# Attention with cluster masks, then token mixing, on one core: last sums read first, late weights cast earlier, first maxima moved

## The chip, the cores and the metric

The kernel runs on one core of one Trainium2 chip. A core has five engines that each work through their own queue in order: TensorE (PE, with its weight loads as PEld), VectorE (DVE), ScalarE (ACT), GpSimd (POOL) and SyncE (SP), which here issues nearly all DMAs. The metric is the device time of one execution in microseconds. Times in the text are microseconds unless marked otherwise.

## What is computed

Two steps, the second on the output of the first. B = 4, H = 8 heads, S = 768 tokens, D = 64, 16 clusters, so the second step has a model width of 512.

```python
q_assign = argmax(q_n . c_n);  k_assign = argmax(k_n . c_n)      # cluster of each query and key
mask   = q_assign[:, :, :, None] == k_assign[:, :, None, :]
scores = where(mask, scale * q @ k.T, -1e9)
attn   = exp(scores - max(scores));  attn /= sum(attn) + 1e-9
x      = (attn @ v) as [B, S, 512]

theta  = x @ w_theta
yr     = einsum('ts,bsd->btd', w_tok_r, x * cos(theta))
yi     = einsum('ts,bsd->btd', w_tok_i, x * sin(theta))
u      = x + yr + yi
out    = u + maximum(u @ w_ch, 0)
```

## The kernel before, in words

**Precision.** Large products are made from a high and a low part. A ScalarE copy rounds a tensor to its high part (`hi`, type fp32r), GpSimd or VectorE subtracts it from the whole for the low part (`lo`), and TensorE adds three products: hi by hi, hi by lo, lo by hi. The weights arrive as 64-bit floats and are turned into 32-bit ones first (`to_f32`, L124): one ScalarE operation (L142), then four on VectorE (L144, L147, L150, L153). `split_w` (L157) does that and the split (L165, L166).

**Attention.** A pair is two heads of one batch on the two halves of the partitions; there are 16 pairs, `NPAIR`. A unit `u` is one block of 128 keys against one half (384) of the queries, for both heads `j` of the pair; a pair has 12 units, 192 in all (`NUT`). For each unit: `score_products` makes the scores on TensorE (L408, four products: three of the split and one with the mask rows `mk`, `mq`), `exps` takes the exponential on ScalarE (`at`, L471), `add_exps` sums on GpSimd (L482), and `weighted` multiplies by `v` (L543). Ten units ahead (`LEAD`) `max_products` computes whole rows of scores (tile `m`, two PSUM buffers, one for each head) and `max_of` takes their maximum on VectorE (`nm`, L430); `shift_row` brings it into a row of `mq` by a small DMA (L451). `interleave` issues several lists of products in turn, `both` makes the two heads' products in turn and then calls a function for each head.

The cluster of each token is found per pair: logits (L286), turned (`lt`, L299), maximum and one-hot code on VectorE, turned back (`ot`, L327). Pairs 0 and 1 do that ahead of the loop. `keep_up(n)` issues n small matmuls that compute nothing anybody reads (L228, tile `idle`); `WAIT` gives their numbers at five places: ahead of and behind the turn of the centroids (L254, L256), ahead of the turns of the logits (L724), ahead of the one-hot codes (L731) and ahead of the loop (L760).

The end of a pair has two generators, driven by unit numbers. `sums` (L499) adds up the exponentials by a product with a column of ones (tile `sm`, L510), reads the result (for the last pair `last_sum`, VectorE, L518, tile `se`), sends it through DRAM and back, takes the reciprocal (L528) and loads it broadcast (`rb`). `normalise` (L560) multiplies the pair's output by it (L564, for the last two pairs on VectorE) and stores it. Pair `pi` has its steps at units `12 pi + 12 + SUMS` and `12 pi + 12 + NORM`. So the last product of sums (pair 15) stands at unit 196, and pair 14 is normalised at units 193 and 196.

**Token mixing.** A tile is 128 tokens of a batch, 6 in each, 24 in all. `theta(b, t)` computes the angles (tile `tp`, L643), reduces them modulo 2 pi on VectorE (`rotation_reduce`: `kk` L648, `r` L649 and L650), takes cosine and sine on ScalarE and multiplies by x (L911, L913), and splits the results into `zhc, zlc, zhs, zls` (ScalarE L916, GpSimd L918). `mix` adds the tile's products with the token weights into six PSUM banks `y` (L967). A tile's `theta` is written two tiles ahead of its `mix` (`AHEAD`). After the sixth tile of a batch `channel` adds x (`add_y`, L978, split at L980 and L981) and multiplies by `w_ch` (`channel_out`, tiles `cp` and `cy`, L990). x as rows arrives by `xb` loads (L631), one buffer, turned on VectorE (L636).

The token weights of row blocks 0 to 2 are ready in split form from the attention stage. Those of blocks 3 to 5 are kept in DRAM as 32-bit floats, and `w_ch` (blocks c0 to c3) is converted in the second stage. The generator `late` (L870) does both; the loop over tiles takes one step of it in each of the six tiles of batch 0. The block casts (L878) are held behind a split that `weights_after` names, and all their temporary tiles are the four buffers of tag `u` that `add_y` uses later.

**What sets the order.** In the attention stage the order on every engine is the program's, tied by hand with `in_order` (L673). In the second stage a planner orders each engine's queue by program order and by times that it estimates, except where `behind(x)` or `issue_after` holds an instruction behind x on the same engine. The second stage's PSUM pools (`pm` with two banks, `py` with the six y banks) take over the banks of the attention's pools, the one of the last `sm` among them.

Of the kernel before, what the change touches and what calls it, by code (L numbers as in the profile page):

```python
# [23 lines left out]
TAIL = 2  # L24
NEXT = 6
FILL = 5
WAIT = (37, 10, 11, 28, 14)
SUMS = (4, 6, 8, 9, 10)
NORM = (13, 16)
TERMS = 3  # L30
# [4 lines left out]
INV_2PI = float(1.0 / (2.0 * math.pi))  # L35
# [8 lines left out]
def kernel(  # L44
# [19 lines left out]
    nc = tc.nc  # L64
# [3 lines left out]
    NT = S // P  # L68
# [156 lines left out]
    def keep_up(n, over=None):  # L225
        over = idle if over is None else over
        for _ in range(n):
            nc.tensor.matmul(over[:, 0:P], lhsT=busy, rhs=busy, start=True, stop=True)  # L228
# [174 lines left out]
    def interleave(*lists):  # L403

        for x in zip(*lists):
            for j, (out, stat, cols, mov, over, start, stop) in x:
                r = slice(64 * j, 64 * j + 64)
                nc.tensor.matmul(out, lhsT=stat[r, cols], rhs=mov[r, over], start=start, stop=stop)  # L408

    def max_products(u, j):  # L410

        pi, a, i = split_u(u)
        s = st[pi]
        if i == 0 and ("nm", a) not in s:
            s["nm", a] = p2.tile([P, 2, NH], F32, tag="nm", name=f"nm{u}")
        t = a * NH + i // 2
        m = s["m", j] = m_tile(f"m{u}_{j}")
        q = slice(t * P, (t + 1) * P)
        res = []
        for c in range(2):  # L420
            k = slice(c * HS, (c + 1) * HS)
            res.append((j, (m[:, c, 0:HS], s["hq"], q, s["hk"], k, True, False)))
            res.append((j, (m[:, c, 0:HS], s["mq"], q, s["mk"], k, False, True)))
        return res

    def max_of(u, j):

        pi, a, i = split_u(u)
        s = st[pi]
        nc.vector.tensor_reduce(  # L430
            out=s["nm", a][:, j, i // 2:i // 2 + 1], in_=s["m", j][:, :, 0:HS], op=ALU.max, axis=AX.XY,
            negate=True)
# [55 lines left out]
    def both(products, u, then, *banks):  # L488
        interleave(*(products(u, j, *banks) for j in range(2)))
        for j in range(2):  # L490
            then(u, j)
# [68 lines left out]
    def normalise(pi):  # L560
        b, p = divmod(pi, NP)
        s = st.pop(pi)

        (nc.gpsimd if pi < NPAIR - 2 else nc.vector).tensor_tensor(  # L564
            out=s["xt"], in0=s["xt"], in1=s["rb"], op=ALU.mult)
        yield
        nc.sync.dma_start(out=xT_d[b][:, p], in_=s["xt"].rearrange("p a s -> p (a s)"))
# [13 lines left out]
    def run(gen):  # L581
        for _ in gen:
            pass
# [28 lines left out]
    def behind(x):  # L612
        return tc.issue_after(x.ins) if x is not None else nullcontext()
# [31 lines left out]

    def rotation_reduce(n, name, tp, kk, r):

        nc.vector.tensor_scalar_mul(kk, tp, INV_2PI)  # L648
        nc.vector.scalar_tensor_tensor(out=r, in0=kk, scalar=-C1, in1=tp, op0=ALU.mult, op1=ALU.add)  # L649
        nc.vector.scalar_tensor_tensor(out=r, in0=kk, scalar=-C2, in1=r, op0=ALU.mult, op1=ALU.add)  # L650
        ab = ma[n % 2].tile([P, DM], F32, tag="ab", name=f"ab{name}")
        with behind(first_sin[0] if n == 1 else None):
            nc.scalar.activation(out=ab, in_=r, func=AF.Abs)
        return ab
# [7 lines left out]
    def stages(units, gen):  # L662

        for u in units:
            at_unit(u, lambda: next(gen, None))
        at_unit(units[-1] + 1, run, gen)
# [95 lines left out]
    for pi in range(NPAIR):  # L762
        u = NU * pi
        if pi > 0:
            prepare(pi, g2 if pi == 2 else assign(pi))
            at_unit(u - NU + 7, load_v, pi)
        for a in range(2):
            if pi or a:
                at_unit(u + a * NT - LEAD + NT, shift_row, pi, a)
        if pi < NPAIR - 1:  # L770
            for a in range(2):
                at_unit(7 if pi == a == 0 else u + ADDS[a], add_sums, pi, a)
        stages([u + NU + k for k in SUMS], sums(pi))
        stages([u + NU + k for k in NORM], normalise(pi))
    for x, gen in enumerate(early_weights()):
        units = [W_EVERY * x + k for k in W_UNITS]
        stages(units if units[-1] < NUT else W_LAST[x % (NPAIR - 1)], gen)
# [4 lines left out]
    u = 0  # L782
    while u <= NUT or todo:
        start = len(nc.cur_bb.bb.instructions)
        ahead = u + LEAD

        def pieces(u):
            for x in sorted(x for x in todo if x <= u):
                for fn, a in todo.pop(x):
                    fn(*a)  # L790

        if 0 <= u < NUT:
            both(score_products, u, exps)
            if u == 0:
                for n, x in ((1, "mk"), (0, "mq")):
                    nc.scalar.activation(
                        out=st[1][x], in_=turn_one_hot(1, n), func=AF.Identity,
                        **(dict(scale=BIG, bias=mbi) if n else {}))
                nc.gpsimd.memset(cl["q"], -100.0)
                keep_up(NEXT)  # L800
                both(max_products, ahead - 2, max_of)
                keep_up(2 * NEXT)
            add_exps(u)
            if ahead < NUT:
                scores_beside_max(u + 1, ahead, 0)
        pieces(u - 0.5)
        if 0 < u <= NUT:
            weighted(u - 2)
            if u == NUT:
                keep_up(FILL, m_tile("fill")[:, 0])  # L810
            weighted(u - 1)
            if ahead >= NUT:
                weighted_out(u - 1)
        pieces(u)
        if 0 <= u < NUT:
            if ahead < NUT:
                scores_beside_max(u + 1, ahead, 1)
            else:

                both(score_products, u + 1, exps, *([m_tile(f"sc{u + 1}")] if u < NUT - 6 else []))  # L820
            add_exps(u + 1)
        if 0 < u and ahead < NUT:
            weighted_out(u - 1)
        pieces(u + 1)
        in_order(start)
        u += 2
# [43 lines left out]
    def late():  # L870

        for t in range(EARLY, NT):
            for w, x in ((w_r, "r"), (w_i, "i")):
                hi, lo = w[t]
                kept = u_tile("kept").rearrange("p c s -> p (c s)").bitcast(F32)[:, 0:S]
                nc.sync.dma_start(out=kept, in_=w_d[t, x])
                with behind(weights_after[0]):
                    nc.scalar.copy(out=hi, in_=kept)  # L878
                nc.gpsimd.tensor_tensor(out=lo, in0=kept, in1=f(hi), op=ALU.subtract)
            if t < NT - 1:  # L880
                yield
        for c in range(NCT):
            if c:
                yield
            for gen in split_w(*w_c[c], w_ch[c * P:(c + 1) * P], DM, wt_pair, nc.gpsimd, CK):
                run(gen)

    zs, splits = {}, []

# [209 lines left out]
```

## Time and profile before

| what | value |
|---|---|
| runs of the kernel, median (lowest to highest) | 792.14 (790.19 to 792.31) |
| the profiled execution: device time | 791.57 |
| the profiled execution: span of its instructions | 789.8 |
| mean granted TensorE clock | 0.996 |
| DMA queue share of 16 engines | 30.7% |

The profile was taken on one execution; its span runs from the first to the last instruction, and its device time is a little longer. A row of the timeline gives start, duration, engine, line and operation, with `out<-in`, the shapes, and the number of instructions merged in it; the bracket at the end is the idle time of that engine just before and what ended it. A row of the waits gives who waited for whom, the total, how often, and the longest. A row of the windows gives the length, then the busy time and count of PE, PEld, DVE, ACT and POOL, the granted TensorE clock (1.00 is full), the share of the DMA engines and the GB/s.

The stages lie as follows: start up to about 24, attention up to about 446, mixing from 453, the channel product of batch 0 from 519 to 539 and that of batch 1 from 606 to 623.

### The profile page before, as it was taken

What the parts mean: (1) busy time and instruction counts of PE and PEld (TensorE: products, weight loads), DVE (VectorE), ACT (ScalarE), POOL (GpSimd) and SP (SyncE); (2) the same over time, 40 slices, a digit from 0 to 9 for tenths busy, and PEclk for the clock granted to TensorE, in tenths of its full rate; (3) what the DMA queues carried; (4) which work ended last, traced back from release to release, by engine and by line L of the source; (5) the groups of instructions that cost most, each with busy time, mean ns of one, the idle gap of its engine ahead of it and who ended that gap; (6) DMA issues with size and microseconds to landing.
All of it is one profiled execution on the core that took longest, in us unless ns stands there. A gap on an engine that the chain in (4) does not pass through costs nothing.

```text
span 789.8 us, 14483 instructions
## 1 busy us (share of the span) xinstructions
PE 779.1 (99%) x5624; PEld 577.9 (73%) x5624; DVE 570.7 (72%) x689; ACT 387.8 (49%) x780; POOL 496.2 (63%) x289
## 2 busy tenths in 40 slices
PE   9999999999999999999999899999999999999998
PEld 7666565566565666656665588888889988899998
DVE  6689999999999999999899668754444433633322
ACT  3465756576767676666655445432333123403310
POOL 3468888989999999988987475451216022332231
PEclk9999999999999999999999999999999999999999
DMA  4113314431443234433463575115111411030001
GB/s 142 37 64 99 113 54 133 132 112 66 149 133 113 89 125 139 127 106 127 132 206 105 133 217 152 21 21 173 17 23 28 160 28 27 15 94 14 1 21 61
DMA packets 81708, 73.24 MB, mean 93 GB/s; under 512 B 59544, under 2 KB 65512, under 8 KB 81256
## 3 DMA queue, kind: packets, MB, share of 16 engines
q1 hardware_dynamic: 81634, 72.32, 30.7%
q8 instruction: 44, 0.72, 0.4%
q14 instruction: 24, 0.20, 0.1%
q10 hardware_dynamic: 6, 0.00, 0.0%
HBM read 56.89 MB, written 15.31 MB: 91 GB/s over the span
## 4 chain that ended last, share of the span: by engine, by line
PE 82%; DVE 10%; DMA 3%; issue 2%; ACT 2%; SPq 1%; DVEq 0%; ACTq 0%
PE sc L408 24%; PE y L967 19%; PE av L543 15%; PE tp L643 6%; PE cy L990 5%; PE m L408 4%; PE cp L990 3%; DMA xb<-xT_d 2%; PE sm L510 1%; PE lg L286 1%; PE idle L228 1%; DVE nm L430 1%; PE y L990 1%; DVE acc L486 1%; PE lt L299 1%
## 5 line engine op out<-in xcount | busy, mean ns | idle before, releaser
L471 ACT ACTIVATE at<-sc 128x384 f32<-128x384 f32 x384 | 173.7, 493 | 99.8 <-PE sc L408 50.8
L430 DVE TENSOR_REDUCE nm<-m 128x1 f32<-128x768 f32 x192 | 179.7, 945 | 21.9 <-PE m L408 19.2
L482 POOL TENSOR_TENSOR acc<-at,at 128x768 f32<-128x768 f32 x64 | 129.0, 2016 | 36.7 <-ACT at L471 33.6
L408 PE MATMUL m<-hk,hq 64*128 64x384 f32 x384 | 146.8, 385 | 0.8 <-DVE nm L430 0.6
L543 PE MATMUL av<-at,vt 128*64 128x384 f32 x768 | 145.3, 499 | 0.2 <-ACT xt L558 0.2
L918 POOL TENSOR_TENSOR zlc<-ab,zhc 128x512 fp32r<-128x512 f32 x24 | 32.3, 1345 | 169.3 <-ACT zhc L916 165.8
L482 POOL TENSOR_TENSOR acc<-acc,at 128x768 f32<-128x768 f32 x64 | 131.9, 2061 | 7.9 <-ACT at L471 5.7
L408 PE MATMUL m<-mk,mq 64*128 64x384 f32 x384 | 127.3, 334 | 0.0
L408 PE MATMUL sc<-hq,hk 64*128 64x384 f32 x384 | 117.0, 387 | 0.9 <-ACT at L471 0.9
L408 PEld LDWEIGHTS sc<-hq,hk 64*128 64x128 f32 x384 | 56.1, 183 | 61.7 <-issue 24.9
L408 PE MATMUL sc<-lq,hk 64*128 64x384 f32 x384 | 98.1, 335 | 0.0
L408 PE MATMUL sc<-mq,mk 64*128 64x384 f32 x384 | 98.0, 335 | 0.0
L408 PE MATMUL sc<-hq,lk 64*128 64x384 f32 x384 | 97.8, 334 | 0.0
L543 PEld LDWEIGHTS av<-at,vt 128*64 128x64 f32 x768 | 46.5, 136 | 58.5 <-issue 53.6
L408 PEld LDWEIGHTS m<-hk,hq 64*128 64x128 f32 x384 | 70.1, 183 | 3.1 <-DVE nm L430 2.3
L408 PEld LDWEIGHTS m<-mk,mq 64*128 64x128 f32 x384 | 70.7, 185 | 0.2 <-DVE mk L714 0.2
L648 DVE TENSOR_SCALAR kk<-tp 128x512 int32<-128x512 f32 x24 | 16.4, 684 | 73.4 <-PE tp L643 73.2
L486 DVE TENSOR_TENSOR acc<-acc,acc 128x768 f32<-128x768 f32 x30 | 68.9, 2295 | 0.0
L616 ACT CAST xh<-xT 128x512 fp32r<-128x512 f32 x23 | 14.3, 620 | 99.1 <-PE tp L643 99.1
L981 POOL TENSOR_TENSOR ul<-xT,uh 128x384 fp32r<-128x384 f32 (+1 forms) x36 | 33.5, 960 | 37.2 <-ACT uh L980 35.5
L408 PEld LDWEIGHTS sc<-mq,mk 64*128 64x128 f32 x384 | 55.1, 184 | 0.0
L408 PEld LDWEIGHTS sc<-lq,hk 64*128 64x128 f32 x384 | 55.1, 185 | 0.0
(174 smaller groups left out, 1728.0 us busy)
## 6 DMA issues: line engine op xcount, KB each, us to landing
vt<-in_v_dram SPq DMA_DIRECT2D x16, 384.0 KB
rb<-sd SPq DMA_DIRECT2D x32, 192.0 KB
xT_d<-xt SPq DMA_DIRECT2D x16, 384.0 KB
xb<-xT_d SPq DMA_DIRECT2D x96, 64.0 KB
rawq<-in_qT_dram SPq DMA_DIRECT2D x15, 384.0 KB
rawk<-in_kT_dram SPq DMA_DIRECT2D x15, 384.0 KB
w<-in_wrT_dram SPq DMA_DIRECT2D x6, 768.0 KB
xT<-xT_d SPq DMA_DIRECT2D x3, 1536.0 KB
```

The costliest lines, as they stand in the source:

```text
L408: nc.tensor.matmul(out, lhsT=stat[r, cols], rhs=mov[r, over], start=start, stop=stop)
L430: nc.vector.tensor_reduce(out=s["nm", a][:, j, i // 2:i // 2 + 1], in_=s["m", j][:, :, 0:HS], op=ALU.max, axis=AX.XY, negate=True)
L471: last_exp[0] = nc.scalar.activation(out=s["at", a, i][:, j], in_=s["sc", j], func=AF.Exp, scale=SCALE)
L482: last_acc[0] = nc.gpsimd.tensor_tensor(out=s["acc", a, x], in0=prev, in1=at, op=ALU.add)
L486: nc.vector.tensor_tensor(out=s["acc", a, 0], in0=s["acc", a, 0], in1=s["acc", a, 1], op=ALU.add)
L543: nc.tensor.matmul(s["av"][64 * j:64 * j + 64], lhsT=s["vt"][:, i, j, :], rhs=s["at", a, i][:, j], start=(i == 0), stop=(i == NT - 1))
L643: nc.tensor.matmul(tp, lhsT=xx[:, c, :], rhs=w_th[c][k], start=(n == 0), stop=(n == 3 * NCT - 1))
L648: nc.vector.tensor_scalar_mul(kk, tp, INV_2PI)
L918: nc.gpsimd.tensor_tensor(out=zl, in0=tr, in1=zh.bitcast(F32), op=ALU.subtract)
L967: last_mix[0] = nc.tensor.matmul(y_at(b, d, c0, c1), lhsT=zz[:, d * P:(d + 1) * P], rhs=ww[:, c0:c1], start=first and lead, stop=last, ski ...
L981: nc.gpsimd.tensor_tensor(out=ul[:, d, :], in0=x, in1=uh[:, d, :].bitcast(F32), op=ALU.subtract)
L990: nc.tensor.matmul(cp, lhsT=w_c[d][k][:, e * P:(e + 1) * P], rhs=uu[:, d, :], start=(n == 0), stop=(n == 3 * NCT - 1), skip_group_check=True)
```

## The change

Five edits, in three places of the program.

- The end of attention: `kk` of token tile 1 is held behind `last_sum` on VectorE, and `normalise` of pair 14 moves four units later, to units 197 and 200, behind the last pair's product and its read at unit 196.
- The late weights: `late` yields at other points. Row blocks 3 and 4 come in tile 0 (before: 3 in tile 0, 4 in tile 1), block 5 and c0 in tile 1 (before tile 2), c1, c2 and c3 in tiles 2, 3 and 4 (before 3, 4 and 5), and tile 5 has none.
- The start: in unit 0 the maxima of unit 8 are issued right behind the first scores, one head after the other, ahead of the turns of pair 1's one-hot codes; before, they came behind those turns and were interleaved. The 6 + 12 filler matmuls around them go, and three numbers of `WAIT` fall: 10 to 4, 11 to 9 and 14 to 8.

```diff
-WAIT = (37, 10, 11, 28, 14)
+WAIT = (37, 4, 9, 28, 8)
...
-        nc.vector.tensor_scalar_mul(kk, tp, INV_2PI)
+        with behind(last_sum[0] if n == 1 else None):
+            nc.vector.tensor_scalar_mul(kk, tp, INV_2PI)
...
-        stages([u + NU + k for k in NORM], normalise(pi))
+        stages([u + NU + k + (4 if pi == NPAIR - 2 else 0) for k in NORM], normalise(pi))
...
             both(score_products, u, exps)
             if u == 0:
+                for j in range(2):
+                    interleave(max_products(ahead - 2, j))
+                    max_of(ahead - 2, j)
                 for n, x in ((1, "mk"), (0, "mq")):
                     nc.scalar.activation(
                         out=st[1][x], in_=turn_one_hot(1, n), func=AF.Identity,
                         **(dict(scale=BIG, bias=mbi) if n else {}))
                 nc.gpsimd.memset(cl["q"], -100.0)
-                keep_up(NEXT)
-                both(max_products, ahead - 2, max_of)
-                keep_up(2 * NEXT)
...
-            if t < NT - 1:
+            if t == NT - 2:
                 yield
         for c in range(NCT):
-            if c:
-                yield
             for gen in split_w(*w_c[c], w_ch[c * P:(c + 1) * P], DM, wt_pair, nc.gpsimd, CK):
                 run(gen)
+            yield
```

## The prediction

> **What bounds the kernel now.** I read the chain that ended last first, then TensorE's waits, and only then single stretches of the timeline. The page's part 4 by engine, and two rows of the waits of TensorE:
>
> ```profile
> PE 82%; DVE 10%; DMA 3%; issue 2%; ACT 2%; SPq 1%; DVEq 0%; ACTq 0%
> PE y L967 <- DVE se L518: 2.3, 1, 2.3
> PE cy L990 <- ACT uh L980: 1.3, 1, 1.3
> ```
>
> The end is set by TensorE: it is on 82% of the chain, and no other engine comes near it. So an edit is worth only what it takes off TensorE: an idle gap, a stretch at a low clock, or instructions. Two single gaps stand out, 2.3 us at the first token-mixing product and 1.3 us in the first channel product. They cost more than their length, as the granted clock (the figure before the DMA share) shows in one slice behind each:
>
> ```profile
> 454.00:455.00 1.00, 1.00 (x5) 0.81 (x4) 1.00 (x3) 0.97 (x3) 0.00 (x0) 0.50 1.02 406
> 523.00:524.00 1.00, 1.00 (x5) 1.00 (x4) 1.00 (x4) 0.92 (x4) 1.00 (x2) 0.50 0.09 16
> ```
>
> TensorE is fully busy in both slices, at half its clock. A gap here is paid twice, once idle and once slow.
>
> **Part 1: the last sums, and the multiplication kk of token tile 1 behind them.** TensorE and VectorE where attention ends and mixing begins, the start of the next tile's theta product, and a later mixing of one tile from the chain:
>
> ```profile
> 446.18 1.50 PE L510 MATMUL sm<-acc,ecol 128*32 128x384 f32 x16
> 447.43 2.05 DVE L564 TENSOR_TENSOR xt<-xt,rb 128x768 f32<-128x768 f32 x1
> 449.40 0.68 DVE L648 TENSOR_SCALAR kk<-tp 128x512 int32<-128x512 f32 x1
> 449.59 1.08 PE L643 MATMUL tp<-wth_hi,xl 128*128 128x512 f32 x4
> 452.30 0.54 DVE L518 TENSOR_SCALAR se<-sm 128x384 f32<-128x384 f32 x1
> 452.99 0.58 PE L967 MATMUL y<-wr_hi,zhc 128*128 128x512 f32 x2 [2.32 <-DVE se L518]
> 463.02 1.08 PE L643 MATMUL tp<-wth_hi,xh 128*128 128x512 f32 x4
> 542.03 8.41 PE y L967 x48
> ```
>
> The sums are ready at 446.18 + 1.50 = 447.68, but VectorE reads them (se) only at 452.30: normalise of pair 14 (2.05), kk and what hangs on it stand ahead. The PSUM banks of y lie over the attention's pools, so the first y waits for that read, although TensorE is free at 449.59 + 1.08 = 450.67. The change puts pair 14's normalise at units 197 and 200, behind the last product at unit 196, and kk behind se. Then se runs at about 447.9, or 0.7 to 1.2 later if an instruction of tile 3 is put in ahead; either way it is done before 450.67. The 2.32 of idle time goes, and the slow clock with it: mixing tile 0 takes 463.02 - 452.99 = 10.03 against 8.41 later on, 1.62 more. Gain 2.32 + 1.62 = 3.94. Bounds: 0 (another reader of those banks, or the low halves of tile 0, come as late as se) to 3.94.
>
> What is late next: the same VectorE work is still to be done, with se first. VectorE is free for it from 447.43 and has to wait for the sums, 0.3 to 0.5, and kk, r and all of tile 1's halves move back by that. TensorE meets tile 1 earlier:
>
> ```profile
> 458.36 1.30 POOL L918 TENSOR_TENSOR zls<-r,zhs 128x512 fp32r<-128x512 f32 x1
> 465.76 0.50 PE L967 MATMUL y<-wr_hi,zhc 128*128 128x512 f32 x2
> ```
>
> Tile 1's last half is done at 459.66, then about 460.1; its mixing starts at 465.76 - 3.94 = 461.8. That is 1.7 to spare, so I cost it at nothing. With that cover gone, each us late is a us, and about 1.6 of low clock on top.
>
> Here the Trainium skill ("TensorE: Matmul & The Clock Gate", the section on why this matters for your kernels) advises against idle gaps over about 3 us, since one idle window takes the clock back to half. The gaps of 2.32 and 1.30 above are shorter and still have 0.50 behind them, so the trace decides, and I give the rule no chance here; by it idle time alone would count, 2.32 + 1.30 + the 0.8 of part 3 = 4.4 and 787.7, in place of the sum below.
>
> **Part 2: the late weights.** Each of tiles 0 to 5 of batch 0 has a share of the late weights: before t3 / t4 / t5 and c0 / c1 / c2 / c3, after t3 and t4 / t5 and c0 / c1 / c2 / c3 / none (t: the two token weights of a row block, c: a block of w_ch). Nothing is added or removed; c1 to c3, t4, t5 and c0 come one tile earlier. The last tile before the channel product is then free. The channel product of batch 0 beside that of batch 1, with the VectorE work ahead of each:
>
> ```profile
> 511.51 1.40 DVE L147 TENSOR_SCALAR wtmp<-wtmp 128x512 int32<-128x512 int32 x1
> 517.44 0.74 DVE L978 TENSOR_TENSOR xT<-y,xT 128x384 f32<-128x384 f32 x2
> 518.78 0.51 PE L990 MATMUL cp<-uh,wch_hi 128*128 128x384 f32 x2
> 521.24 0.45 PE L990 MATMUL cy<-uh,wch_hi 128*128 128x384 f32 x1 [1.30 <-ACT uh L980]
> 539.10 1.08 PE L643 MATMUL tp<-wth_hi,xh 128*128 128x512 f32 x4
> 599.82 0.76 DVE L978 TENSOR_TENSOR xT<-y,xT 128x384 f32<-128x384 f32 x2
> 606.04 0.51 PE L990 MATMUL cp<-uh,wch_hi 128*128 128x384 f32 x2
> 622.70 1.08 PE L643 MATMUL tp<-wth_hi,xh 128*128 128x512 f32 x4
> ```
>
> In batch 1, which has no weights to convert, the first sum x + y (L978) starts 606.04 - 599.82 = 6.22 ahead of the channel product; in batch 0 only 518.78 - 517.44 = 1.34, because the conversion of c3 stands in VectorE's queue. So the casts uh come late, TensorE idles 1.30 and then runs slow. The same matmuls take 539.10 - 518.78 = 20.32 in batch 0 and 622.70 - 606.04 = 16.66 in batch 1. Without c3 there, batch 0 should look like batch 1: gain 3.66, bounds 0 and 3.66.
>
> What this crowds is tiles 0 to 2: ScalarE gets two casts and GpSimd two subtractions more right behind tile 1, on SP the loads for t5 and c0 wait for buffers that are freed there, and the xb loads of a later tile stand behind them. Tiles are made about two ahead of their mixing, which covers it; the case where it doesn't is the slower rival.
>
> **Part 3: the start.** Pair 0's first units, then what stands before them:
>
> ```profile
> 23.23 0.95 PE L228 MATMUL idle<-busy 128*128 128x128 bf16 x14
> 24.11 0.44 PE L408 MATMUL sc<-hq,hk 64*128 64x384 f32 x2
> 25.01 1.13 PE L327 MATMUL ot<-identb,clq 128*128 128x128 bf16 x12
> 25.86 0.90 ACT L796 ACTIVATE mk<-ot,mbi 128x768 fp32r<-128x768 bf16 x1
> 26.41 0.44 PE L408 MATMUL m<-hk,hq 64*128 64x384 f32 x2
> 27.32 0.84 PE L228 MATMUL idle<-busy 128*128 128x128 bf16 x12
> 28.09 0.44 PE L408 MATMUL sc<-hq,hk 64*128 64x384 f32 x1
> 28.43 0.44 PE L408 MATMUL m<-hk,hq 64*128 64x384 f32 x1
> 29.28 0.49 ACT L471 ACTIVATE at<-sc 128x384 f32<-128x384 f32 x1 [1.81 <-PE sc L408]
> 7.18 0.11 PEld L286 LDWEIGHTS lg<-rawk,cb 128*32 128x32 f32 x1 [0.59 <-DMA rawk<-in_kT_dram]
> 7.96 0.79 PE L228 MATMUL idle<-busy 128*128 128x128 bf16 x11
> 8.11 0.48 ACT L290 COPY lgs<-lg 128x384 f32<-128x384 f32 x1
> ```
>
> Fourteen fillers take 24.11 - 23.23 = 0.88; six fewer are 0.35 to 0.4, so the first scores start at about 23.75 if the rows of mq that a DMA writes are there by then (at 24.4 for the fourth product); if not, this part is worth nothing. Then come the maxima of unit 8, now one head after the other: the pair takes 27.32 - 26.41 = 0.91, and a head alone occupies its rows as long, so 1.8. The twelve turns come after them, at 23.75 + 0.9 + 1.8 = 26.45 in place of 25.01, and next scores at about 27.2 instead of 28.09. TensorE gains 0.9, but mk and mq on ScalarE wait for the turns: mk starts at about 26.95 in place of 25.86, mq ends at about 28.5, and the next exponential follows there, 0.8 before the 29.28 of now. From there ScalarE sets the pace for a few us, so I take 0.8; bounds 0 and 1.3 (TensorE's own gain with the 0.34 that it now waits for the maxima, 28.09 to 28.43). What follows is tied to this by order and by data, so the shift stays to the end.
>
> The other fillers lie under waits: the 4 in place of 10 end before a load that lets TensorE go on at 7.18, and 9 in place of 11 before the copy lgs that ends at 8.59. Both 0.
>
> **Sum.** 3.94 + 3.66 + 0.8 = 8.4. The profiled execution took 791.57 with a span of 789.8, so 783.2 for such an execution; the median 792.14 of the three runs lies 0.57 above it, and I forecast 783.7.
>
> **The rivals.** (a) The channel stall stays, because the order on VectorE and ScalarE is planned ahead and may still put x + y late: gain 3.94 + 0.8, 787.4. For it: the turn of that order is not mine to see. Against: batch 1 has the same work there and no stall. (b) The y products find another wait in place of se, so part 1 is worth 0: 787.6. Against: the waits name se, and nothing later reads those banks.
>
> (c) The clock comes up late at the start: the six fillers removed at 5.3 leave a hole in TensorE's first busy stretch, and at the low clock logits, turns and fillers up to 10 us take longer:
>
> ```profile
> 5.26 1.27 PE L228 MATMUL idle<-busy 128*128 128x128 bf16 x10
> ```
>
> A filler is 0.127 here and 0.79 / 11 = 0.07 at 7.96, so the clock rises between the two. Late, it would add about 0.8 to the chain of logits and maxima and eat part 3: 784.5. The Trainium skill's page on the clock gate, same section, asks for 4 us of continuous work to bring the clock up; by it this hole could matter.
>
> (d) Slower: crowding on GpSimd. If t3, t4 and c0 are queued there ahead of tile 2's low halves, tile 2 waits for the conversion of c0:
>
> ```profile
> L879 POOL TENSOR_TENSOR wi_lo<-kept,wi_hi 128x768 fp32r<-128x768 f32 x3 | 7.2, 2387 | 0.0
> 473.68 2.87 SPq L136 DMA_DIRECT2D wtmp<-in_w_ch_dram  x2
> 479.45 0.67 ACT L142 ACTIVATE wtmp<-wtmp 128x512 f32<-128x512 f32 x1 [1.12 <-DMA wtmp<-in_w_ch_dram]
> 486.84 1.38 POOL L166 TENSOR_TENSOR wch_lo<-wtmp,wch_hi 128x512 fp32r<-128x512 f32 x1 [4.35 <-ACT wch_hi L165]
> ```
>
> Three such subtractions at up to 2.39 from 460.1 free c0's buffer at about 467, its load and chain take 486.84 + 1.38 - 473.68 = 14.5, tile 2's halves (2 x 1.3) end at about 484, and the first of them would be wanted at about 461.8 + 11.15 + 0.7 = 473.7 (11.15 = 8.41 and the theta product, 465.76 - 463.02). A wait of about 9 with 1.6 of slow clock is 10.6, against 8.4 gained: 794.3. It decides from about 7 us of wait on. Against it: tile 2 is written ahead of these in the program, and its inputs are ready long before c0's. (e) Nothing much comes of any part: the freed time turns up as other waits, 791.
>
> **Chances.** Forecast 0.56, (a) 0.14, (b) 0.10, (c) 0.08, (d) 0.05, (e) 0.07. The range takes in forecast, (a), (b) and (c), with 1 us for the spread of the runs (790.19 to 792.31) and the bounds of part 3: 781.3 to 788.6. A measurement here can tell about 0.3%, 2.4 us. Faster than that are the forecast and (a) to (c): 0.88; within it (e) and half of (d): 0.09; slower the rest: 0.03.
>
> **What would show it.** Right: no wait of y for se, se within 1.5 us of the end of sm, a clock of 1.00 throughout mixing tile 0 and the first channel product, that product 16.7 long, and the first y about 2.32 + 0.8 = 3.1 earlier than 452.99. Wrong: y waiting for another name, a new wait for tile 1's or 2's halves, a channel product still near 20, or fillers before 10 us at 0.1 each.

## The result

| what | before | changed |
|---|---|---|
| runs on one chip, median (lowest to highest), 4 each | 791.16 (789.74 to 792.31) | 783.28 (783.12 to 783.5) |
| the profiled execution: device time | 791.57 | 783.16 |
| the profiled execution: span of its instructions | 789.8 | 781.4 |
| mean granted TensorE clock | 0.996 | 1.000 |

The medians differ by 7.88; the ratio is 0.9901, with a 95% interval of 0.9881 to 0.9922. (The kernel before has one run more here than in the table ahead of the prediction.) The span of the profiled execution fell by 8.4, which is the sum that was forecast. Its terms were not all as forecast, and the experiments below show that they do not simply add.

The chain of the changed kernel by engine, and then two waits of TensorE, the longest one and that of y for se (total, times, longest):

```profile
PE 92%; DVE 4%; DMA 1%; issue 1%; SPq 1%; ACT 1%; POOL 0%; DVEq 0%
```

```profile
PE idle L228 <- DVE ecol L113: 1.1, 1, 1.1
PE y L967 <- DVE se L518: 0.5, 1, 0.5
```

TensorE's part of the chain went from 82% to 92%. Of the two gaps that the prediction named, the one of cy for uh is gone from the list of waits, and the one of y for se is down from 2.3 to 0.5.

Three places of the changed kernel's timeline: the end of the start, the end of attention with the first token-mixing product, and the channel product of batch 0:

```profile
6.64 0.68 PE L228 MATMUL idle<-busy 128*128 128x128 bf16 x9
7.34 0.55 PE L299 MATMUL lt<-identf,lgs 128*128 128x128 f32 x3
22.92 0.45 PE L408 MATMUL sc<-hq,hk 64*128 64x384 f32 x2
26.15 0.90 ACT L800 ACTIVATE mk<-ot,mbi 128x768 fp32r<-128x768 bf16 x1 [1.33 <-PE ot L327]
444.76 1.50 PE L510 MATMUL sm<-acc,ecol 128*32 128x384 f32 x16
446.13 1.69 DVE L618 TENSOR_TENSOR xl<-xT,xh 128x512 fp32r<-128x512 f32 x1
448.49 0.71 DVE L636 STREAM_TRANSPOSE xn<-xb 128x512 f32<-128x512 f32 x1 [0.67 <-DMA xb<-xT_d]
449.12 0.52 DVE L518 TENSOR_SCALAR se<-sm 128x384 f32<-128x384 f32 x1
449.79 0.59 PE L967 MATMUL y<-wr_hi,zhc 128*128 128x512 f32 x2 [0.54 <-DVE se L518]
458.28 1.08 PE L643 MATMUL tp<-wth_hi,xh 128*128 128x512 f32 x4
508.66 0.74 DVE L978 TENSOR_TENSOR xT<-y,xT 128x384 f32<-128x384 f32 x2
514.05 0.51 PE L990 MATMUL cp<-uh,wch_hi 128*128 128x384 f32 x2
530.71 1.08 PE L643 MATMUL tp<-wth_hi,xh 128*128 128x512 f32 x4
```

Read from mark to mark, the 8.4 splits like this. Up to sm: 446.18 against 444.76, so 1.42. From sm to the theta product behind mixing tile 0: 463.02 - 446.18 = 16.84 before, 458.28 - 444.76 = 13.52 now, so 3.32. The five mixings in between, with their theta products, take the same time in both (55.76 and 55.77). The channel product: 20.32 before, 530.71 - 514.05 = 16.66 now, so 3.66. Two windows of the changed kernel, mixing tile 0 and the channel product, show the granted clock (the figure before the DMA share) full in both:

```profile
449.00:463.00 14.00, 13.46 (x73) 11.42 (x72) 11.50 (x17) 9.42 (x15) 7.08 (x4) 1.00 0.69 193
514.00:531.00 17.00, 17.00 (x99) 16.92 (x99) 5.18 (x13) 2.06 (x5) 8.05 (x8) 1.00 0.30 87
```

### The profile page after: what moved, and what is told of

The parts are those of the page before. It is cut to its first block, busy times and chain, and to the rows that moved or that the text cites. A ratio compares the mean times of both kernels' runs of the same rounds, so it can differ in the third digit from the quotient of the medians.

```text
span 781.4 us, 14422 instructions
## 1 busy us (share of the span) xinstructions
PE 773.2 (99%) x5592; PEld 573.0 (73%) x5592; DVE 567.8 (73%) x689; ACT 388.2 (50%) x780; POOL 500.6 (64%) x289
## 4 chain that ended last, share of the span: by engine, by line
PE 92%; DVE 4%; DMA 1%; issue 1%; SPq 1%; ACT 1%; POOL 0%; DVEq 0%
PE y L967 26%; PE sc L408 25%; PE av L543 15%; PE tp L643 7%; PE cy L990 5%; PE m L408 4%; PE cp L990 3%; PE lg L286 1%; PE sm L510 1%; PE y L990 1%; PE lt L299 1%; DVE acc L486 1%; DVE mk L373 1%; PE mt L438 1%; DVE nm L430 1%
## 5 line engine op out<-in xcount | busy, mean ns | idle before, releaser
L408 PEld LDWEIGHTS sc<-hq,lk 64*128 64x128 f32 x384 | 55.2, 184 | 0.0
```

## The experiments

Two figures are used for each: the stage from sm to the theta product behind mixing tile 0 (16.84 before, 13.52 changed), and the stage from the end of batch 0's mixing to the next theta product. The end of mixing is taken as that first theta product plus 55.76, since those five mixings and theta products ran without a wait in the kernels for which the figure is given. That second stage is 16.66 where nothing waits, as in batch 1. An instruction behind an added line can have a line number a few higher or lower than in the two main kernels.

**One part at a time.** The first four kernels were timed beside the kernel before on one chip, where it took 789.83 (788.99 to 791.87, 24 runs). The first has the start alone:

```diff
-WAIT = (37, 10, 11, 28, 14)
+WAIT = (37, 4, 9, 28, 8)
...
+                for j in range(2):
+                    interleave(max_products(ahead - 2, j))
+                    max_of(ahead - 2, j)
...
-                keep_up(NEXT)
-                both(max_products, ahead - 2, max_of)
-                keep_up(2 * NEXT)
```

> The kernel before with the edits of the start alone (three WAIT numbers, the maxima of unit 8 ahead of the turns, 18 fillers gone). Theory (each part acts alone, and the start is worth what its own rows give): from the first scores of pair 0 to the first product with v 0.4 less than the 7.72 of before, 0.35 to 0.4 from the six fillers ahead of the first scores, 0.8 in all, about 790.4; the gap at y (2.3) and the stall of the channel product (1.3) both stay. Rival (the 1.4 us that the changed kernel is ahead by at the end of attention came from data that happened to land earlier in that one execution, not from the edits): first turns at about 11.8 as before, and no difference in time that five rounds show.

Measured: 788.87, ratio 0.9987 (0.9978 to 0.9995), 0.96 less. The start is worth about what was forecast. Its timeline and a window of mixing tile 0 show something else:

```profile
451.98 0.59 PE L967 MATMUL y<-wr_hi,zhc 128*128 128x512 f32 x2 [2.41 <-DVE se L518]
460.43 1.08 PE L643 MATMUL tp<-wth_hi,xh 128*128 128x512 f32 x4
516.70 0.62 PE L990 MATMUL cp<-uh,wch_hi 128*128 128x384 f32 x2 [0.34 <-ACT uh L980]
519.35 0.62 PE L990 MATMUL cy<-uh,wch_hi 128*128 128x384 f32 x1 [1.30 <-ACT uh L980]
```

```profile
454.00:455.00 1.00, 1.00 (x8) 0.89 (x7) 1.00 (x3) 0.37 (x1) 0.00 (x0) 1.00 1.27 218
```

The gap at the first y is all there, 2.41, but the clock behind it is 1.00, and mixing tile 0 takes 460.43 - 451.98 = 8.45, where the profile before had 10.03. So the slow stretch behind that gap is not a fixed price of it. And the channel product has a new wait of 0.34 ahead of the old one.

The second kernel has the end of attention alone:

```diff
-        nc.vector.tensor_scalar_mul(kk, tp, INV_2PI)
+        with behind(last_sum[0] if n == 1 else None):
+            nc.vector.tensor_scalar_mul(kk, tp, INV_2PI)
...
-        stages([u + NU + k for k in NORM], normalise(pi))
+        stages([u + NU + k + (4 if pi == NPAIR - 2 else 0) for k in NORM], normalise(pi))
```

> The kernel before with the edits at the end of attention alone (kk of tile 1 behind the last sums, pair 14 normalised at units 197 and 200). Theory: from the first sm product to the start of tile 3's theta product 13.5 in place of 16.84, so 3.3 less: about 788.0; granted clock 1.00 throughout; the wait of y for se at 0.5. The channel stall of 1.3 stays, as the late weights are where they were. Rival (the stall depends on where PE stands against the converting engines): with mixing 3.3 us earlier and the conversions no faster the stall grows by some of that, and the gain is 2 or less, about 789.5.

Measured: 788.54, ratio 0.9986 (0.9977 to 0.9995), 1.29 less. The edit does what it says where it stands: y waits 0.95 for se, and the first stage takes 459.61 - 445.76 = 13.85. But the stage of the channel product grew from 20.32 to 537.82 - (459.61 + 55.76) = 22.45, with 0.70 + 1.29 of waits for uh and the rest of it mostly low clock (0.72 on the mean from 514 to 526). ScalarE's timeline has the cast zhs of each tile, at the end of its preparation, and one cast of a block of w_ch:

```profile
484.70 0.63 ACT L917 CAST zhs<-r 128x512 fp32r<-128x512 f32 x1
496.01 0.62 ACT L917 CAST zhs<-r 128x512 fp32r<-128x512 f32 x1
500.67 0.62 ACT L165 CAST wch_hi<-wtmp 128x512 fp32r<-128x512 f32 x1 [3.45 <-DVE wtmp L153]
507.37 0.62 ACT L917 CAST zhs<-r 128x512 fp32r<-128x512 f32 x1
515.68 0.51 ACT L981 CAST uh<-xT 128x384 fp32r<-128x384 f32 x1 [2.50 <-DVE xT L979]
```

The steps are 11.31 and 11.36. TensorE needs 11.15 for a tile (55.76 for five). The steps are not TensorE's own pace: from 485 to 515 ScalarE waits for VectorE alone, as in the row at 500.67, and VectorE for ScalarE alone, neither of them for TensorE. So while there is a block of w_ch to convert in each tile, ScalarE and VectorE prepare tiles no faster than TensorE uses them, and what TensorE gains ahead of that stretch it would lose again where the first uh is needed. That is the theory which the later runs test.

The third kernel has the late weights alone:

```diff
-            if t < NT - 1:
+            if t == NT - 2:
                 yield
         for c in range(NCT):
-            if c:
-                yield
             for gen in split_w(*w_c[c], w_ch[c * P:(c + 1) * P], DM, wt_pair, nc.gpsimd, CK):
                 run(gen)
+            yield
```

> The kernel before with the late weights moved alone. Theory: the channel product of batch 0 takes 16.7 in place of 20.32, no wait of cy for uh; the gap at y stays 2.3 with its slow clock: about 787.5, 3.7 less. Rival (the stall is not the conversion of c3 but the late start of tile 5's own work): the product stays above 19 and the time within 1 of the kernel before.

Measured: 787.18, ratio 0.9965 (0.9952 to 0.9977), 2.65 less. No wait is left in the channel product, and that stage takes 533.82 - (461.15 + 55.76) = 16.91. In this execution too the gap at y was there (2.30 for se) and the clock behind it 1.00: mixing tile 0 took 461.15 - 452.65 = 8.50.

Alone, the three parts are worth 0.96 + 1.29 + 2.65 = 4.9. Together they were worth 7.88 on the first chip and, below, 6.63 on another. By the 95% intervals, which I estimate at 1.4 either way for the 4.9 and at 1.3 for the 6.63, the times alone hardly tell these apart; the stages of the traces do, as the next kernels show.

The fourth kernel measures the gap at y by itself: the kernel before with nothing moved, and one theta product more on TensorE, which fills the gap with work that nobody needs.

```diff
+            if late:
+                rotation_angle(xh, xl, tp)
```

> The kernel before, with the theta product of tile 2 done twice in a row (the second time overwrites the first with the same values), so that TensorE works through the wait for se and the wait itself stays. Theory (the slow stretch after the gap is the price of TensorE standing idle): granted clock 1.00 in mixing tile 0, which takes 8.4 in place of 10.03; the product done again is 2.74 long against 2.32 of gap, so it starts 0.4 later; 1.2 less in all, about 790.0. Rival (the clock falls there for another reason, such as the DMA share above 1.0 or the fp32r products themselves): clock 0.50 as before and 0.4 more than before.

Measured: 792.66, ratio 1.0034 (1.0022 to 1.0046), so 2.8 slower where 790.0 was expected. In the first stage it is as the theory had it: y comes without a wait at 452.72 with the clock full, and the stage takes 461.13 - 445.68 = 15.45, 1.39 less than before. (As two kernels had the clock full behind the gap itself, this does not show that the work in the gap kept it up.) The rest was missed. The channel product waited 2.04 and 1.05 for uh, and its stage took 540.20 - (461.13 + 55.76) = 23.31: against 20.32 before, the 1.39 gained ahead of it was lost there, and 1.6 more.

**Two parts, and all again.** The next four were timed on another chip, where the kernel before took 789.98 (789.04 to 792.38, 11 runs). First the end of attention and the late weights together, without the start (the diffs of the second and third kernel):

> The changed kernel with the start of the kernel before: the parts at the end of attention and of the late weights together. Alone they gave 1.3 and 2.65 on this chip. Theory A (the parts are not independent: with a conversion of w_ch in every tile, VectorE and ScalarE need more than TensorE's 11.15 per tile, so what TensorE gains at the first y is lost again in front of the channel product; the moved weights set it free): more than the sum, 784.2, with a channel product of 16.7 and no wait there. Rival B (independent parts): 785.9, the sum.

Then the changed kernel again:

> The changed kernel itself on this chip, to stand beside the parts. Theory A: 783.2, which is 1.7 or more below what the three parts alone add up to (789.83 - 0.96 - 1.29 - 2.65 = 784.93). Rival B: 784.9.

Measured: 784.63 (ratio 0.9927, 0.9912 to 0.9942) and 783.35 (0.9913, 0.9897 to 0.9929). The end and the late weights together are worth 5.35, against 1.29 + 2.65 = 3.94 alone; the start adds 1.28 to that, against 0.96 alone. So the start adds, and the other two need one another: with the late weights moved, the channel product no longer takes back what the end of attention frees, and no wait is left there (product at 515.61, next theta product at 532.27, 16.66, against 22.45 without them). In the profile without the start, y waited 1.33 for se; in that of the changed kernel on this chip, the channel product waited 0.29 for uh.

**Is more to be had at y?** Two kernels try to remove the last wait for se. In the changed kernel two instructions stand ahead of se on VectorE, xl of tile 3 and xn of tile 2 (446.13 and 448.49 in the fence above). xn of tile 1 runs before them, at 443.17, and that of tile 2 has to follow it, as both are turned out of the one buffer xb. One kernel puts xl of tile 3 and xn of tile 1 behind se, and with the latter xn of tile 2; the other only the turning of x (xn):

```diff
-        rotation_parts(xs, xh, xl, last_out[0] if late else None)
+        rotation_parts(xs, xh, xl, last_out[0] if late else last_sum[0] if n == AHEAD + 1 else None)
...
-        rotation_turn(n, xn)
+        with behind(last_sum[0] if n == 1 else None):
+            rotation_turn(n, xn)
```

> The changed kernel with two more VectorE instructions of later tiles behind the read of the last sums (the turn xn of tile 1, which waits for a load, and the low part xl of tile 3). The read of the sums is then first, and the planner also moves the reciprocal of the last sums ahead of the end of tile 1's reduction. Theory A (the residual wait of 0.54 goes, but the reciprocal waits for two DMAs, 7 after the read, with tile 1's reduction queued behind it): first y with no wait, then a new wait of 1.5 to 3 at the mixing of tile 1, slower than the changed kernel by 1 to 3. Rival B (the read of the sums was the last limit there): 0.5 to 0.7 faster.

> The changed kernel with only the turn xn of tile 1 behind the read of the last sums. The reciprocal then stands behind tile 1's reduction, but ahead of its multiplications. Theory A: first y 0.5 to 0.7 earlier, tile 1's last half at about 461.5 by the marks of the changed kernel where it is wanted at about 461.4, so no wait worth naming: 0.5 faster. Rival B (the reciprocal's wait holds up tile 1 and 2 by over 1): a wait at the mixing of tile 1, no gain or a loss.

Measured: 785.17 (ratio 0.9939, 0.9924 to 0.9954) and 784.52 (0.9927, 0.9912 to 0.9942), so 1.8 and 1.2 slower than the changed kernel on that chip. The wait for se is gone in both, and y starts at 448.83 and 448.60 in place of 449.66. In the second, xl of tile 3 still stands ahead of se and is 1.60 long: so it was the turn that waits for a load of xb, and not xl, that made se late. The time is lost behind it, though not at the mixing of tile 1, where the expectations looked for it and where nothing waits. Rows of the second of the two, VectorE's and then TensorE's:

```profile
475.96 0.71 DVE L636 STREAM_TRANSPOSE xn<-xb 128x512 f32<-128x512 f32 x1 [4.20 <-DMA xb<-xT_d]
511.32 0.74 DVE L979 TENSOR_TENSOR xT<-y,xT 128x384 f32<-128x384 f32 x2
512.78 0.51 PE L991 MATMUL cp<-uh,wch_hi 128*128 128x384 f32 x2
515.12 0.44 PE L991 MATMUL cy<-uh,wch_hi 128*128 128x384 f32 x1 [1.29 <-ACT uh L981]
517.40 0.62 PE L991 MATMUL cp<-uh,wch_hi 128*128 128x384 f32 x2 [0.38 <-ACT uh L981]
```

xb has one buffer. Where xn is read out of it later, the next loads start later, and for tile 4 (475.96) VectorE waits 4.20 for one. The first x + y then comes at 511.32, only 1.46 ahead of the channel product, and 1.29 + 0.38 of waits are back.

**Why the late weights work.** The last four were timed where the kernel before took 790.15 (788.6 to 791.43, 9 runs). The first is the second kernel (end of attention alone) without the conversion arithmetic of w_ch:

```diff
         yield
+        if weights_after[0] is not None:
+            return w
         nc.vector.tensor_scalar(
```

> The kernel before with the edits at the end of attention alone, and the four VectorE steps that turn w_ch into 32-bit floats left out (the loads, the two ScalarE operations and the subtraction stay; the values of w_ch are wrong). With the conversion the product of channel 0 and what hangs on it took 22.44 us from the end of mixing to the next theta product, and 788.54 in all. Theory (the conversions make the loop of ScalarE and VectorE that prepares a tile about as long as TensorE's 11.15 per tile, so that time gained on TensorE ahead of it is lost again at the channel product): without them that stretch takes 16.7, no wait of cy for uh, 782.8 in all. Rival (the stall is of ScalarE's casts or of the last y, not of the conversion): the stretch stays at 20 or more, 787 to 788.5.

Measured: 784.96 (ratio 0.9935, 0.9923 to 0.9948), against 788.54 with the conversion. ScalarE's and TensorE's rows:

```profile
484.26 0.62 ACT L919 CAST zhs<-r 128x512 fp32r<-128x512 f32 x1
492.07 0.62 ACT L919 CAST zhs<-r 128x512 fp32r<-128x512 f32 x1
494.74 0.62 ACT L618 CAST xh<-xT 128x512 fp32r<-128x512 f32 x1 [0.83 <-PE tp L645]
501.11 0.62 ACT L919 CAST zhs<-r 128x512 fp32r<-128x512 f32 x1
515.01 0.51 PE L993 MATMUL cp<-uh,wch_hi 128*128 128x384 f32 x2
531.68 1.09 PE L645 MATMUL tp<-wth_hi,xh 128*128 128x512 f32 x4
```

The tiles are prepared in steps of 7.81 and 9.04 in place of 11.3, and in the second of them ScalarE already waits 0.83 for TensorE, so that the loop is no longer the limit. Nothing waits in the channel product, and its stage is 531.68 - (459.25 + 55.76) = 16.67. That is the theory's figure for the stage. The whole time is 2.2 above the 782.8 that was expected; 1.7 of that is my working, which took the stall of the one profiled execution of the second kernel (790.27) off that kernel's median (788.54).

The second asks whether it is the place of the last conversion that counts, or the total. It is the changed kernel with c3 back in the sixth tile; the fifth has none:

```diff
                 run(gen)
             yield
+            if c == NCT - 2:
+                yield
```

> The changed kernel with one thing put back: the block c3 is converted in the sixth tile again and the fifth has none. Theory of position (what the prediction said: c3 stands in VectorE's queue ahead of x + y): the stall of the channel product is back, cy waits about 1.3 for uh, the stretch from the end of mixing to the next theta product takes 20 to 23 in place of 16.7, 787 in all. Theory of the loop's total (any tile without a conversion gives back about 3.7 us, wherever it stands): the stretch takes 17 to 18, and 783.5 to 784.5 in all.

Measured: 784.81 (ratio 0.9934, 0.9922 to 0.9947). VectorE's and TensorE's rows:

```profile
448.94 0.71 DVE L636 STREAM_TRANSPOSE xn<-xb 128x512 f32<-128x512 f32 x1 [1.45 <-DMA xb<-xT_d]
450.24 0.59 PE L969 MATMUL y<-wr_hi,zhc 128*128 128x512 f32 x2 [1.33 <-DVE se L518]
506.70 0.69 DVE L153 SCALAR_TENSOR_TENSOR wtmp<-wtmp 128x512 int32<-128x512 int32 x1
510.49 0.74 DVE L980 TENSOR_TENSOR xT<-y,xT 128x384 f32<-128x384 f32 x2
514.50 0.51 PE L992 MATMUL cp<-uh,wch_hi 128*128 128x384 f32 x2
531.25 1.08 PE L643 MATMUL tp<-wth_hi,xh 128*128 128x512 f32 x4
```

The conversion of c3 stands in the last tile again, and still nothing waits: 531.25 - 514.50 = 16.75. Its last step starts 510.49 - 506.70 = 3.79 ahead of x + y, as in the kernel before (517.44 - 513.66 = 3.78). Place is not the cause; the free tile ahead of it gave the time back. The profiled execution took 783.71, 0.55 more than that of the changed kernel, and neither theory had the reason: a load of xb came later, xn waited 1.45 for it with se behind it, and y waited 1.33 in place of 0.54. The median is 1.5 above the changed kernel's; the rest of that does not show in the profile, and its cause is open.

The last two move c1 and c2 into one tile, so that two tiles are free, once in the changed kernel and once in the one with xn behind se:

```diff
                 run(gen)
-            yield
+            if c != 1:
+                yield
```

> The changed kernel with c1 and c2 both converted in the third tile and c3 in the fourth, so that two tiles ahead of the channel product are free in place of one. Theory: the changed kernel has next to no wait left there (0 to 0.3), so nothing is to be had: 783.3, within 0.5. Rival (two conversions in one tile make the loop about 3.7 longer there, and a tile's halves come late): a new wait of y of about 2 in the third to fifth tile, 785 to 787.

> The kernel of e8_turn_behind (the turning of x of one more tile held behind the read of the last sums), with c1 and c2 converted in the third tile and c3 in the fourth. In e8_turn_behind the first product of mixing came 1.1 us earlier than in the changed kernel, but 1.66 us of waits in the channel product took it back: 784.52. Theory: with two free tiles the loop has room, those waits go, the stretch from the end of mixing to the next theta product is 16.7 again, and the 1.1 us is kept: 782.2. Rival (the loop is late by other work than the conversions): the waits stay, 784.5.

Measured: 782.79 (ratio 0.9914, 0.9898 to 0.9929) and 783.55 (0.9919, 0.9904 to 0.9933). The first agrees with the theory: nothing that these runs can tell from the changed kernel. (The two medians are from two chips.) In the second the theory fell by half. VectorE's and TensorE's rows:

```profile
476.43 0.71 DVE L636 STREAM_TRANSPOSE xn<-xb 128x512 f32<-128x512 f32 x1 [3.30 <-DMA xb<-xT_d]
510.94 0.74 DVE L980 TENSOR_TENSOR xT<-y,xT 128x384 f32<-128x384 f32 x2
513.48 0.51 PE L992 MATMUL cp<-uh,wch_hi 128*128 128x384 f32 x2
514.74 0.45 PE L992 MATMUL cy<-uh,wch_hi 128*128 128x384 f32 x1 [0.39 <-ACT uh L982]
517.02 0.62 PE L992 MATMUL cp<-uh,wch_hi 128*128 128x384 f32 x2 [0.38 <-ACT uh L982]
```

The waits went from 1.67 to 0.77, not to nothing, and the stage takes 531.70 - 513.48 = 18.22: the wait for the xb load stays, and the freed tiles do not make up for it. No version tried is measurably faster than the changed kernel.

One number goes through all of them: how far the first x + y starts ahead of the channel product.

| kernel | x + y ahead by | waits for uh in the product |
|---|---|---|
| theta product done twice | 1.14 | 2.04 + 1.05 |
| end of attention alone | 1.14 | 0.70 + 1.29 |
| start alone | 1.15 | 0.34 + 1.30 |
| before | 1.34 | 1.30 |
| xn behind se | 1.46 | 1.29 + 0.38 |
| xn and xl behind se | 1.58 | 1.29 + 0.37 |
| xn behind se, two free tiles | 2.54 | 0.39 + 0.38 |
| changed, again | 3.52 | 0.29 |
| late weights alone | 3.86 | none |
| c3 in the last tile | 4.01 | none |
| end of attention and late weights | 5.37 | none |
| changed | 5.39 | none |
| changed, two free tiles | 5.54 | none |
| end of attention alone, no conversion | 6.21 | none |

From 3.9 on nothing waited; at 3.5 and below something did. In the first three rows the channel product itself waited for uh; 1.14 or 1.15 is there what the sum and the cast take, and the room was less than that by the first wait.

## Why the prediction was right, and where not

The prediction was right in sign and in the time that it gave, 783.2 by its sum for the profiled execution against 783.16 measured. By its own steps:

**Part 1, 3.94 forecast, 3.32 found.** "Either way it is done before 450.67" failed, and with it "the 2.32 of idle time goes". I allowed one instruction of tile 3 ahead of se. There were two: xl of tile 3, 1.69 long, and the turn xn of tile 2, which waited until 448.49 for a load of xb. So se ran 449.12 - 446.26 = 2.86 behind the end of sm, and y still waits 0.54. The load set that time, and the prediction's working has no such wait there: with the turns behind se and xl still ahead of it, nothing waited. (TensorE comes to that place 1.42 earlier than in the working, at 449.25.) The second half of the term, 1.62 of slow clock, was in the profile before but does not belong to the gap: with gaps of 2.41 and 2.30 the clock stayed at 1.00 in two executions. That half was luck of the execution from which I read it.

Tile 1 was not late: its last half ends on GpSimd at 458.80, and its mixing starts at 461.02.

**Part 2, 3.66 forecast, 3.66 found.** The figure held, the reason only in part. "Because the conversion of c3 stands in VectorE's queue" is a statement of place, and the kernel with c3 back in that place had no stall. What the runs show in its place is a loop of ScalarE and VectorE that takes 11.3 per tile where each tile has a conversion, and 7.8 to 9.0 without that arithmetic, against TensorE's 11.15. In the kernel before, the casts zhs come at steps of 11.48, 11.18 and 11.36 up to the last tile, so there is no tile in which to catch up. In the changed kernel the steps are 10.26, 11.61, 10.37 and then 7.53 in the free tile; with the fifth tile free they are 10.25, 11.60 and 6.56. One free tile, fifth or sixth, is enough, or nearly: one of two profiles of the changed kernel still has a wait of 0.29.

**Part 3, 0.8 forecast, 1.42 in the profile, 0.96 in the runs of it alone.** The fillers and the order of the maxima come out close: the eight fillers ahead of the first scores take 22.92 - 22.37 = 0.55 where the fourteen took 0.88, 0.33 less, mk follows the first scores by 26.15 - 22.92 = 3.23 where I had 26.95 - 23.75 = 3.20, and the first av product follows them by 7.28 in place of 7.72. That is 0.33 + 0.44 = 0.77. The other 0.65 is what was left at sm of a difference from ahead of the fillers: in the execution before, TensorE waited until 7.18 for a load, lt started at 8.65, 1.31 later than in the changed one, and of that 23.23 - 22.37 = 0.86 was left at the fillers. (From the first av product to sm the changed execution took 0.21 more.) The kernel with the late weights alone, whose start is that of before, has lt at 7.38 and its fillers at 22.36. So "Both 0" for the first two numbers of WAIT stands, and the rest was the load's time in that execution.

**The sum.** -0.62 in part 1 and +0.62 in part 3 cancel. That is chance, and there was a step that I did not write down: that the three terms add. They do not. Part 1 is worth 1.29 alone, where the stage of the channel product grows from 20.32 to 22.45 and takes most of it back, and 5.35 - 2.65 = 2.70 beside part 2 (the 2.65 is from another chip). Had the change been parts 1 and 3 alone, the same way of adding would have said 4.7, and 0.96 + 1.29 = 2.3 is what they gave alone.

**The size of the gain.** The forecast time came out, the gain of 8.4 only for the execution from which it was read. The mean granted clock is on record for executions that were not profiled too: of 44 executions of the kernel before on three other chips, 7 have 1.000, 30 have 0.997 or 0.998, and 7 have 0.995 or 0.996, as the profiled one has. The medians of the three groups are 789.6, 789.8 and 791.6. So the prediction was read from an execution of the rarer kind, with 791.57, and against the usual one the change is worth about 6.5; on the second chip it was 6.63.

**The rivals.** (a), the stall that stays, did not come about in the changed kernel, but it is what the parts without the late weights showed, and stronger than before: "uh late" was a limit behind TensorE's, not a single late instruction. (b), another wait in place of se, and (e), nothing, did not come. (c) did not either: the nine fillers at 6.64 take 0.68, 0.075 each, so the clock was up.

(d), the crowding on GpSimd, came nearer than its chance of 0.05. GpSimd's timeline of the changed kernel, the conversions of row blocks 3 and 4 and then tile 2's low halves:

```profile
458.77 2.29 POOL L880 TENSOR_TENSOR wr_lo<-kept,wr_hi 128x768 fp32r<-128x768 f32 x1
...
465.82 2.30 POOL L880 TENSOR_TENSOR wi_lo<-kept,wi_hi 128x768 fp32r<-128x768 f32 x1
468.07 1.75 POOL L918 TENSOR_TENSOR zlc<-ab,zhc 128x512 fp32r<-128x512 f32 x1
469.78 1.29 POOL L918 TENSOR_TENSOR zls<-r,zhs 128x512 fp32r<-128x512 f32 x1
```

I argued that tile 2 is written ahead of these in the program. On the engine it stands behind four of them. The second ends at 471.07, and TensorE wants it at 473.93, the last of the six kinds of products that begin with the y at 472.18: 2.86 to spare. One more subtraction ahead of it, 2.3, would have left about half a microsecond.

## What to carry to other kernels

When one engine sets the end, ask for each stretch how long the next engine's loop takes per step. Where it is as long as the first engine's, time gained ahead of that stretch is lost at the end of it, and gains on either side of it can't be added; a stretch that lightens the second loop makes the others count. A wait that shows as a single gap may be the end of such a loop: measure the steps of the loop, not the last instruction in it.

A price that is read from one execution (a slow clock behind a gap, a load that came late) should be looked for in a second one before it is put into a sum.

## What the hardware showed that was not expected

A gap on TensorE costs slow clock in some executions and none in others. The windows of the kernel before at both ends of the low stretch behind its gap of 2.32, and of the one behind its gap of 1.30:

```profile
453.00:454.00 1.00, 1.00 (x5) 0.91 (x6) 0.89 (x2) 0.53 (x1) 0.00 (x0) 0.82 1.03 378
457.00:458.00 1.00, 1.00 (x7) 0.84 (x6) 0.24 (x1) 1.00 (x3) 1.00 (x1) 0.97 0.69 53
521.00:522.00 1.00, 0.76 (x3) 0.53 (x4) 1.00 (x3) 1.00 (x4) 0.68 (x1) 0.95 0.00 0
525.00:526.00 1.00, 1.00 (x7) 1.00 (x6) 0.00 (x0) 0.00 (x0) 1.00 (x2) 0.84 0.03 3
```

Between the two of each pair it is 0.50. At half speed, 0.82 puts the start at 453.64 and 0.97 the end at 457.06: 3.42. The second stretch lasts from 521.90 to 525.32, again 3.42. Behind the waits of the channel product the start alone has one of 3.41 (519.45 to 522.86), and the end of attention alone and the theta product done twice have one of 6.83 each, twice as long (518.20 to 525.03 and 520.05 to 526.87). Yet the two kernels that put xn behind se, with all conversions in place as in the changed kernel, have none, with waits of 1.29 + 0.37 and 1.29 + 0.38. The gap of 2.41 in the kernel with the start alone and that of 2.30 with the late weights alone had no such stretch.

The Trainium skill ("TensorE: Matmul & The Clock Gate", the part on the HAM clock gate) says that the clock follows activity in a window of about 3.4 us that runs freely, without regard to the kernel. The lengths of the low stretches agree with that. So does their place: in windows of 0.05 the two of the kernel before are 3.413 long and start at 453.637 and 521.904, 68.267 apart, which is 20 times 3.413. A free window would also make it a matter of where the gap falls. Counted back in steps of 3.413 the gap of the kernel before, 450.67 to 452.99, lies inside one window, 450.22 to 453.64, while the gap of the start alone, 449.57 to 451.98, is cut in two by a boundary at 451.18. That fits, but it is an inference from two profiles: no run here moved a gap within the window, and a profile without a low stretch does not show where its windows lie. The Trainium skill's advice (same page, the section on why this matters for your kernels) is against gaps of over about 3 us; here 2.32 was enough in one execution.

The changed kernel, in whose profile no wait of TensorE is over 1.1, has a mean clock of 0.999 or 1.000 in all its eight executions on two chips, and its four on the first chip spread over 0.4, where the kernel before spreads over 2.6. One low stretch of 3.41 at half speed is 0.002 of the mean clock; I estimate from that that the 0.997 and 0.998 of most executions of the kernel before are one stretch, and the 0.995 and 0.996 two.

The same VectorE instruction on tiles of one shape takes very different times: xl (L618) is 0.68 long in the median of its group and 1.69 at 446.13, where GpSimd works on tiles beside it (from 445.65 on; until then it had been idle for 2.59). What makes it long was not tried by itself, and it is not what made se late.
